# RetNet attention and an MLP mixer on one core: the channel product of batches 1 to 3 by seven quarter products

## The chip, the cores and the metric

The kernel runs on one core of a Trainium2 chip. The metric is the device time of one execution in microseconds, lower is better; the median of three runs of the kernel before is 209.35 us (208.44 to 210.75). The engines are named as the profile names them: PE (matrix products, with PEld for its weight loads), DVE (vector), ACT (scalar), POOL (GpSimd) and SP, which only issues transfers.

## The reference

For 4 batches, 8 heads, 768 positions and a head size of 64, a recurrent attention with decay, then a mixer over tokens and one over channels:

```python
for t in range(S):                                   # S = 768
    state = gamma * state + einsum('bhd,bhe->bhde', k[:, :, t], v[:, :, t])
    y[:, :, t] = scale * einsum('bhd,bhde->bhe', q[:, :, t], state)
x  = y as (4, 768, 512)
h  = relu(x^T @ w_tok1) @ w_tok2                     # 768 -> 256 -> 768
u  = x + h^T
out = u + relu(u @ w_ch1) @ w_ch2                    # 512 -> 1536 -> 512
```

Inputs and output are float32; the products run in float16 with float32 sums.

## The kernel before

The recurrence is done by chunks of 128 positions, six to a batch. Two heads form a pair, and a batch has four pairs. `front(b, p)` is the attention of one pair and its share of the token mixer. It casts k (scaled by the decay, L471 on ACT or L473 on DVE) and q (L480 or L482), turns both so that the head size lies across partitions (for batches 0 and 1 by PE, L506, with copies out of the bank on L515 and L519; for batches 2 and 3 by a transposing transfer on SP, L497), and forms five state products for each of two heads (L542, 64x64 each, in one bank). A scan on DVE (L547) runs the decay over the five chunks, with the factors in the constant `gsc`; its result U has the chunk index innermost. The two heads' diagonal blocks are copied, scaled, into the f16 tile r (L558 on ACT, L560 on POOL). Scores (L579) are masked on DVE (L593), then L607 (state) and L610 (scores) form y. It is scaled into X (L623 on ACT, L627 on DVE), cast (L640), multiplied by w_tok1 (L651) and w_tok2 (L712), added into X (L719 on DVE), cast again (L727) and turned into uT (SP, L736; for batch 1 by PE, L746 and L752). Batch 0 takes a shorter way to uT (L681, L684, L691).

`back(b)` is the channel mixer. `widen(sh)` multiplies half a batch (384 positions) by w_ch1: 12 column tiles of 4 products of 384 columns (L781), each followed by a relu into the f16 tile h2 on ACT (L797). `narrow(sh)` multiplies by w_ch2: for each tile of 128 positions 12 products of 512 columns in one bank (L818; batch 0 adds its token mixer there, L816), then one DVE addition of X and the bank into a tile `o` (L827), which ACT's queue writes out (L833).

Nothing runs in the order in which it is written. Each piece of work is an `Op` with the engines that can do it and a cost for each. `arrange` plays all of them through a plan with these costs, with a model of the transfer rings (`Rings`) and of buffers and PSUM banks, and picks for each engine in turn the ready Op of the highest priority. The plan's order is then recorded, so each engine has a fixed order of instructions; what is waited for at run time follows from the tiles. An Op's `after` holds it back in the plan alone. In gaps of the plan's first 30 us, PE gets filler products of zeros (L881).

Transfers of k and q are issued on SP (L421, L418), those of v (L429) and the weights (L397, in order w_tok1, w_tok2, three thirds of w_ch1, three of w_ch2) on POOL. Eight PSUM banks are shared: 0 to 4 for the fronts of batches 1 to 3, 5 to 7 for their backs; batch 0 has its own ranges.

Of the kernel before, what the change touches and what calls it, by code (L numbers as in the profile page):

```python
# [40 lines left out]
class Rings:  # L41
# [5 lines left out]
    LAND = dict(SP=750, POOL=900, ACT=1500)  # L47
# [37 lines left out]
def arrange(ops, BUFS, BANKS, rank, fixed=None, noise=None):  # L85
# [87 lines left out]
    while left:  # L173
        moved = False
        wake = INF
        for e in ENGINES:
# [5 lines left out]
            for o in w_:  # L182
# [15 lines left out]
                if fixed is not None:  # L198
                    way = way_fix[o.n]
                else:  # L200
                    way = None
                    for w in o.ways:
                        f = max(t, free[w[0]]) + w[2]
                        if way is None or f < way[0] or (f == way[0] and w[0] == e):
                            way = (f, w)
                    if way[1][0] != e:
                        continue
                    way = way[1]
# [49 lines left out]
def kernel(  # L258
# [31 lines left out]
    BUFS = dict(kf=4, qf=3, k16=3, q16=3, v16=6, kT=4, qT=4, U=2, r16=3, am=8, X=3, x16=5, h1=5, u16=3,  # L290
                uT=3, h2=2, o=4)
    BANKS = dict(first=range(0, 7), front=range(0, 5), back=range(5, 8), back0=range(3, 8))
    XB = 2
# [33 lines left out]
    gsc = const_p.tile([P, NP, (NC - 1) * D], FP, name="gsc")  # L327
# [32 lines left out]
    def emit():  # L360
        nc.vector.memset(mask1, 1.0)
        nc.vector.memset(gsc, 0.0)
        for p in range(NP):
            g = gsc[:, p].rearrange("p (e c) -> p e c", c=NC - 1)
            nc.vector.memset(g[:D, :, 1:], g128[2 * p])
            nc.vector.memset(g[D:, :, 1:], g128[2 * p + 1])
    gp_op = prep("DVE", 4200, emit, prio=(0, -1, 1))
# [13 lines left out]
    NW = 3  # L381
    FW = NF // NW
    wc1 = [const_p.tile([P, NP, FW * P], F16, name=f"wc1_{i}") for i in range(NW)]
    wc2 = [const_p.tile([P, FW, C], F16, name=f"wc2_{i}") for i in range(NW)]
# [4 lines left out]
    def request(prio, cost, emit, dma, takes=()):  # L389
        o = Op(ops, prio, [("POOL", cost, cost, emit)], [], takes, dma=dma,  # L390
               after=queue[-6:-5], behind=queue[-1] if queue else None)
# [14 lines left out]
    rows = []  # L406

    def load(b, p):
        got = []
        for tag, src in (("kf", k), ("qf", q)):  # L410
            s = Slot(tag)
            wide = b < XB and tag == "qf"

            def emit(s=s, src=src, tag=tag, wide=wide):
                t = tile_of(s, [P, 2, NC, D], FP)
                r = src[b, 2 * p:2 * p + 2]
# [3 lines left out]
                else:  # L420
                    nc.sync.dma_start(out=t, in_=r.rearrange("h (c p) d -> p (h c) d", p=P))  # L421
            o = Op(ops, (0, b, p), [("SP", 500, 500, emit)], [], [s], dma=(16, 66) if wide else (96, 18),
                   after=rows[-4:-3] if b == 0 else rows[-2:-1], behind=rows[-1] if rows else None)
            rows.append(o)
            got.append((s, o))
        s = Slot("v16")

        def emit(s=s):
            nc.gpsimd.dma_start(out=tile_of(s, [P, 2, NC, D], F16),  # L429
                                in_=v[b, 2 * p:2 * p + 2].rearrange("h (c p) d -> p (h c) d", p=P))  # L430
        got.append((s, request((0, b, p), 1030, emit, (96, 17), [s])))
        loads[b, p] = got

    def front(b, p):
# [24 lines left out]
        (KF, kd), (QF, qd), (V, vl) = loads[b, p]  # L459
# [33 lines left out]
        def turn(src, dst, dep):  # L493
            if b >= XB:
# [40 lines left out]
        ST, US, RS = Slot(FA), Slot("U"), Slot("r16")  # L535
        EC = (NC - 1) * D

        def emit():
            st = tile_of(ST, [P, 512], FP)[:, :EC].rearrange("p (e c) -> p c e", c=NC - 1)
            for c in range(NC - 1):  # L540
                for j in range(2):
                    nc.tensor.matmul(st[j * D:(j + 1) * D, c], K.tile[:, c, j], V.tile[:, j, c],  # L542
                                     start=True, stop=True)
        pp = op(one("PE", (350, 500), emit), kl + [vl, two_before], [ST], [K, V])

        def emit():
            nc.vector.tensor_tensor_scan(out=tile_of(US, [P, EC], FP), data0=gsc[:, p], data1=ST.tile[:, :EC],  # L547
                                         initial=0.0, op0=ALU.mult, op1=ALU.add)
        prev = op(one("DVE", (740, 820), emit), [pp, gp_op], [US], [ST])

        def emit(e, j):
# [4 lines left out]
            u = US.tile[r].rearrange("p (e c) -> p c e", c=NC - 1)  # L556
# [5 lines left out]
        r0 = op(either(lambda e, f=emit: f(e, 0), ACT=(365, 470), POOL=(400, 470)),  # L562
                [prev, r16_op], [RS], [US])
        r1 = op(either(lambda e, f=emit: f(e, 1), ACT=(365, 470), POOL=(400, 470)),
# [16 lines left out]
        if first:  # L581
            a2 = [op(one("PE", (290, 420), lambda f=emit, h=hf: f([h])), [kt[hf], qt[hf], two_before],
                     A4[2 * hf:2 * hf + 2], [KT, QT]) for hf in range(2)]
        else:
            a2 = 2 * [op(one("PE", (460, 590), lambda f=emit: f([0, 1])), kt + qt + [two_before], A4, [KT, QT])]
# [146 lines left out]
        if b >= XB:  # L732
# [27 lines left out]
    def back(b):  # L760
# [10 lines left out]
        def widen(sh):  # L771
            H2 = H2s[sh]
            rel = []
            for ft in range(NF):
# [11 lines left out]
                for part in cuts:  # L786
# [3 lines left out]
                            [uT_done[b, p, sh] for p in ps_] + [wops["c1", ft // FW], c1],  # L790
# [13 lines left out]
        def narrow(sh):  # L804
            H2, rel = H2s[sh], rels[sh]
            for i in range(HC):
                A, O = Slot(BA), Slot("o")
                last = None
                t = slice((sh * HC + i) * P, (sh * HC + i + 1) * P)
                for f0 in range(0, NF, 2):  # L810
                    def emit(f0=f0, i=i, A=A, H2=H2, t=t):
# [5 lines left out]
                        for ft in range(f0, f0 + 2):  # L817
                            nc.tensor.matmul(A.tile, H2.tile[:, ft, i * P:(i + 1) * P],  # L818
                                             wc2[ft // FW][:, ft % FW],
# [5 lines left out]
                def emit(sh=sh, i=i, A=A, O=O):  # L825
                    o = tile_of(O, [P, C], FP)
                    nc.vector.tensor_tensor(o, X.tile[:, sh * HC + i], A.tile, ALU.add)  # L827
                ad = op(one("DVE", (606, 690), emit), [last] + [x_done[b, p, sh] for p in range(NP)],
                        [O], [A, X])

                def emit(sh=sh, i=i, O=O):
                    t0 = (sh * HC + i) * P
                    nc.scalar.dma_start(out=out[b, t0:t0 + P, :], in_=O.tile)  # L833
# [80 lines left out]
```

## Time and profile before

| | |
|---|---|
| median of 3 runs | 209.35 us (208.44 to 210.75) |
| the profiled execution | 210.22 us, of which the profile's span is 208.5 |
| PE, DVE, ACT, POOL busy | 197.6, 104.7, 103.3, 62.9 us |
| narrow product, L818 | 288 products of 128x512 |
| widening, L781 | 384 products of 128x384 |
| states, L542 | 160 products of 128x64 |
| final addition, L827 | 24 of 128x512 on DVE, 683 ns each |
| scan, L547 | 16 of 128x320 on DVE, 814 ns each |
| HBM | 26.74 MB read, 6.29 MB written |

In the profile an engine's busy time is the time in which it had an instruction under way. A product's duration (379 ns for 512 columns) is longer than its distance from the next in an unbroken stream, since products overlap; the chain of work in order of time shows that distance. Times of stages are counted from the span's start.

### The profile page before, as it was taken

How to read it: one execution, taken by the hardware profiler on the slowest of the kernel's cores; microseconds unless marked ns; L12 is line 12 of the kernel's file. 1: busy time of each engine (PE TensorE's matmuls, PEld its weight loads, DVE VectorE, ACT ScalarE, POOL GpSimd, SP SyncE). 2: the span in 40 equal slices, each digit the busy share in tenths (PEclk: the TensorE clock that was granted, in tenths of full speed). 3: DMA queues.
4: the chain of work that ended last, by engine and by line, in shares of the span. 5: the costliest groups of instructions: out<-in, count | busy, mean ns of one | idle time of the engine just before them, and what ended most of it. 6: DMA issues, size and time to landing. Idle time of an engine off the chain costs nothing.

```text
span 208.5 us, 4578 instructions
## 1 busy us (share of the span) xinstructions
PE 197.6 (95%) x1856; PEld 121.9 (58%) x1856; DVE 104.7 (50%) x218; ACT 103.3 (50%) x210; POOL 62.9 (30%) x100
## 2 busy tenths in 40 slices
PE   7987499999999999999999999999999999999992
PEld 3655387666456677575557666666755545545540
DVE  6988642401468997863747658748441021021021
ACT  2676457677415876356306673566304704704600
POOL 8644362705123457253414225133410000000000
PEclk9999969999999999999999999999999999999998
DMA  6999999999999999999999999972053012012012
GB/s 166 202 198 189 213 197 229 197 226 190 195 173 198 170 197 165 179 213 216 145 225 152 205 133 214 247 177 41 0 119 108 3 50 101 3 50 101 0 50 101
DMA packets 91156, 30.96 MB, mean 148 GB/s; under 512 B 81920, under 2 KB 88064, under 8 KB 91136
## 3 DMA queue, kind: packets, MB, share of 16 engines
q1 hardware_dynamic: 58624, 17.31, 52.9%
q0 software_dynamic: 29056, 7.08, 34.5%
q10 hardware_dynamic: 3456, 6.29, 8.4%
q8 instruction: 14, 0.23, 0.5%
q14 instruction: 6, 0.05, 0.1%
HBM read 26.74 MB, written 6.29 MB: 158 GB/s over the span
## 4 chain that ended last, share of the span: by engine, by line
PE 81%; DMA 10%; DVE 3%; ACT 1%; POOL 1%; SPq 1%; issue 1%; DVEq 0%; POOLq 0%; ACTq 0%
PE bank L781 29%; PE bank L818 29%; DMA qf<-in_q_dram 10%; PE bank L651 5%; PE bank L712 3%; PE bank L579 3%; PE bank L542 2%; PE bank L610 2%; PE bank L607 2%; PE bank L506 2%; PE bank L681 1%; PE bank L816 1%; DVE am L593 1%; POOL r L560 1%; DVE U L547 1%; ACT r L558 1%
## 5 line engine op out<-in xcount | busy, mean ns | idle before, releaser
L797 ACT ACTIVATE h<-bank 128x384 f16<-128x384 f32 x96 | 46.5, 490 | 52.7 <-PE bank L781 27.6
L818 PE MATMUL bank<-wc,h 128*128 128x512 f16 x288 | 68.6, 379 | 0.0
L781 PE MATMUL bank<-uT,wc 128*128 128x384 f16 x384 | 67.7, 326 | 0.0
L781 PEld LDWEIGHTS <-wc 128*128 128x128 f16 x384 | 35.9, 98 | 22.9
L818 PEld LDWEIGHTS <-h 128*128 128x128 f16 x288 | 26.4, 98 | 27.8
L827 DVE TENSOR_TENSOR o<-X,bank 128x512 f32<-128x512 f32 x24 | 16.4, 683 | 47.2 <-PE bank L818 46.9
L593 DVE TENSOR_TENSOR am<-bank,mask 128x384 f16<-128x384 f32 x64 | 31.8, 549 | 16.5 <-PE bank L579 16.3
L558 ACT ACTIVATE r<-U 64x320 f16<-64x320 f32 x24 | 18.8, 782 | 10.7 <-DVE U L547 10.3
L640 POOL CAST x<-X 128x384 f16<-128x384 f32 x26 | 13.3, 512 | 32.9 <-DVE X L627 21.9
L719 DVE TENSOR_TENSOR X<-X,bank 128x384 f32<-128x384 f32 x24 | 12.2, 549 | 12.1 <-PE bank L712 12.0
L482 POOL CAST q<-qf 128x768 f16<-128x768 f32 (+1 forms) x13 | 10.6, 812 | 21.8 <-DMA qf<-in_q_dram 21.8
L429 POOL DMA_DIRECT2D v<-in_v_dram x16 | 16.6, 1039 | 1.9 <-PE bank L610 1.5
L727 POOL CAST u<-X 128x384 f16<-128x384 f32 x21 | 10.2, 508 | 22.6 <-DVE X L719 22.6
L623 ACT ACTIVATE X<-bank,gy 128x192 f32<-128x192 f32 x28 | 10.2, 416 | 10.3 <-PE bank L610 10.2
L610 PE MATMUL bank<-v,am 128*128 128x64 f16 x192 | 15.2, 195 | 0.1
L610 PEld LDWEIGHTS <-am 128*128 128x128 f16 x192 | 12.9, 99 | 3.4 <-DVE am L593 0.7
L547 DVE TENSOR_TENSOR_SCAN U<-gsc,bank 128x320 f32<-128x320 f32 x16 | 13.0, 814 | 1.8 <-PE bank L542 1.4
L881 PE MATMUL bank<-zero 128*128 128x384 f16 x52 | 12.6, 390 | 1.2 <-DVE zero L339 1.2
L651 PE MATMUL bank<-x,wt 128*128 128x128 f16 x192 | 13.7, 224 | 0.0
L651 PEld LDWEIGHTS <-wt 128*128 128x128 f16 x192 | 12.2, 101 | 2.2
L627 DVE TENSOR_TENSOR X<-bank,gyw 128x384 f32<-128x384 f32 x18 | 9.9, 552 | 6.5 <-PE bank L610 6.4
L607 PE MATMUL bank<-r,qT 128*128 128x128 f16 x80 | 12.7, 222 | 0.1
(60 smaller groups left out, 161.7 us busy)
## 6 DMA issues: line engine op xcount, KB each, us to landing
kf<-in_k_dram SPq DMA_DIRECT2D x16, 384.0 KB, 9.1
qf<-in_q_dram SPq DMA_DIRECT2D x16, 384.0 KB, 9.6
out_dram<-o ACTq DMA_DIRECT2D x24, 256.0 KB, 3.3
v<-in_v_dram POOLq DMA_DIRECT2D x16, 192.0 KB, 11.9
wc<-in_moe_w_ch_dram POOLq DMA_DIRECT2D x6, 512.0 KB, 19.8
wt<-in_moe_w_tok_dram POOLq DMA_DIRECT2D x2, 384.0 KB, 19.6
kT<-k SPq DMA_TRANSPOSE x8, 5.9
qT<-q SPq DMA_TRANSPOSE x8, 6.2
```

The costliest lines, as they stand in the source:

```text
L429: nc.gpsimd.dma_start(out=tile_of(s, [P, 2, NC, D], F16), in_=v[b, 2 * p:2 * p + 2].rearrange("h (c p) d -> p (h c) d", p=P))
L547: nc.vector.tensor_tensor_scan(out=tile_of(US, [P, EC], FP), data0=gsc[:, p], data1=ST.tile[:, :EC], initial=0.0, op0=ALU.mult, op1=ALU.add)
L558: nc.scalar.mul(RS.tile[r, :, r], u, g128[2 * p + j])
L593: nc.vector.tensor_tensor(am, src, m, ALU.mult)
L607: nc.tensor.matmul(o, QT.tile[:, c * P:(c + 1) * P], R[:, c - 1], start=True, stop=False)
L610: nc.tensor.matmul(o[:, j * D:(j + 1) * D], AM[2 * hf + j].tile[:, i], V.tile[:, j, c], start=(c == 0), stop=(c == 0 or j == 1))
L640: (nc.vector if e == "DVE" else nc.gpsimd).tensor_copy(X16.tile[:, half(hf)], X.tile[:, half(hf), pc])
L651: nc.tensor.matmul(acc[:, jt * P:(jt + 1) * P], wt1[:, i, jt * P:(jt + 1) * P], X16.tile[:, i], start=(i == 0), stop=(i == NC - 1))
L781: nc.tensor.matmul(acc[:, :SH], w[:, ct, (ft % FW) * P:(ft % FW + 1) * P], UT.tile[:, ct, sh * SH:(sh + 1) * SH], start=(ct == 0), stop=(c ...
L797: nc.scalar.activation(H2.tile[:, ft], A.tile[:, :SH], AF.Relu)
L818: nc.tensor.matmul(A.tile, H2.tile[:, ft, i * P:(i + 1) * P], wc2[ft // FW][:, ft % FW], start=(ft == 0 and b > 0), stop=(ft == NF - 1))
L827: nc.vector.tensor_tensor(o, X.tile[:, sh * HC + i], A.tile, ALU.add)
```

## The change

It has six parts.

1. Seven products. For batches 1 to 3, `narrow7(i0, i1)` takes two tiles of 128 positions together. With their h2 tiles cut in two along the 1536 channels and w_ch2 cut in two both ways, the result is a 2x2 by 2x2 product of blocks, done by seven block products with sums of blocks ahead and behind (Winograd's form of Strassen's method). A block product is 6 products of 256 columns (new L873). Ahead stand four sums of h2 blocks (f16, 128x768, DVE or POOL, new L858), and once in the kernel four sums of w_ch2 blocks (`wsum`, 128x1536, new L979). Behind stand eleven additions of 128x256 (new L889) and one copy on ACT (new L907) for a pair of tiles. Two block products share a bank, and the second is issued after the first has been read.
2. States. The five chunks' products are of the whole array, both heads' k by both heads' v (128x128, new L540); the blocks off the diagonal are formed and not used. They take two banks. The scan is replaced by a copy and four dependent multiply-adds of 128x128 (new L546, L548), U has the chunk index outermost, and `gsc` (3.3 us of memsets) gives way to one column a pair.
3. Outputs are summed in place in X, and written from there; the tiles `o` are gone.
4. w_ch1 comes in pieces of 2, 2, 4 and 4 column tiles instead of 4, 4 and 4. In the plan alone, the first k of batch 1 is held back until the third piece has landed.
5. Buffers: v16 4 (was 6), x16 4 (5), uT 2 (3). Banks of the fronts 0 to 5, of the backs 4 to 7, so that two are shared.
6. The plan's costs: later landings, 400 ns added on DVE after 30 us where it chooses between engines, and a few costs of products.

By the order of the recorded instructions this moves, beside what the parts name: k casts from DVE to ACT (DVE 14 to 8), copies kT likewise (8 to 1), the scaling of y into X (DVE 18 to 7), and each uT transposition on SP one or two places back. PE's 92 widening products of batch 0 stand in one stretch, with batch 1's first turns behind them instead of between them.

The core of the difference, cut:

```diff
-    LAND = dict(SP=750, POOL=900, ACT=1500)
+    LAND = dict(SP=900, POOL=1300, ACT=1500)
...
-                        f = max(t, free[w[0]]) + w[2]
+                        f = max(t, free[w[0]]) + w[2] + (400 if w[0] == "DVE" and t > 30000 else 0)
...
-    BANKS = dict(first=range(0, 7), front=range(0, 5), back=range(5, 8), back0=range(3, 8))
+    BANKS = dict(first=range(0, 7), front=range(0, 6), back=range(4, 8), back0=range(3, 8))
+    SEVEN = (1, 2, 3)
...
+    CW = [2, 2, 4, 4]
+    wsum = const_p.tile([P, 4, K2, N2], F16, name="wsum")
...
             for c in range(NC - 1):
-                for j in range(2):
-                    nc.tensor.matmul(st[j * D:(j + 1) * D, c], K.tile[:, c, j], V.tile[:, j, c],
-                                     start=True, stop=True)
+                nc.tensor.matmul(st[c // 4][:, c % 4 * P:(c % 4 + 1) * P],
+                                 K.tile[:, c].rearrange("p h d -> p (h d)"), V.tile[:, :, c], start=True, stop=True)
...
-            nc.vector.tensor_tensor_scan(out=tile_of(US, [P, EC], FP), data0=gsc[:, p], data1=ST.tile[:, :EC],
-                                         initial=0.0, op0=ALU.mult, op1=ALU.add)
+            nc.vector.tensor_copy(u[:, 0], ST[0].tile[:, :P])
+            for c in range(1, NC - 1):
+                nc.vector.scalar_tensor_tensor(out=u[:, c], in0=u[:, c - 1], scalar=gp[:, p:p + 1],
+                                               in1=ST[c // 4].tile[:, c % 4 * P:(c % 4 + 1) * P],
+                                               op0=ALU.mult, op1=ALU.add)
...
+            sums = [(lambda: h(hb, tb, 0), lambda: h(hb, tb, 1), ALU.add, rb, None),
+                    (lambda: HS.tile[:, 0], lambda: h(ha, ta, 0), ALU.subtract, ra[:K2], 0),
+                    (lambda: h(ha, ta, 0), lambda: h(hb, tb, 0), ALU.subtract, ra[:K2] + rb[:K2], None),
+                    (lambda: h(ha, ta, 1), lambda: HS.tile[:, 1], ALU.subtract, ra[K2:], 1)]
...
+                    for j in range(K2):
+                        nc.tensor.matmul(acc[:, half], l[:, j], r[:, j], start=(j == 0), stop=(j == K2 - 1))
...
+            p1 = product(0, lo, lambda: h(ha, ta, 0), w(0, lo), ra[:K2] + cw)
+            u0 = op(either(emit, ACT=act(N2), DVE=dve(N2)), [p1], [US], [banks[0]])
+            p2 = product(2, lo, lambda: h(ha, ta, 1), w(1, lo), ra[K2:] + cw)
+            y1 = add(part(x0, lo), part(x0, lo), u(0), [u0] + xd, [US, X])
+            o11 = add(part(x0, lo), part(x0, lo), acc(2, lo), [p2, y1], [X, banks[2]])
+            p6 = product(0, hi, lambda: HS.tile[:, 1], t(1), [sm[1], u0] + wsums)
+            u2 = add(u(1), u(0), acc(0, hi), [u0, p6], [US, banks[0]])
+            p5 = product(1, lo, lambda: HS.tile[:, 0], t(0), [sm[0]] + wsums)
+            y3 = add(part(x1, lo), part(x1, lo), u(1), [u2] + xd, [US, X])
+            p4 = product(2, hi, lambda: h(hb, tb, 1), t(3), rb[K2:] + wsums + [o11])
+            u4 = add(u(2), u(1), acc(1, lo), [u2, p5], [US, banks[1]])
+            z3 = add(part(x1, lo), part(x1, lo), acc(2, hi), [p4, y3], [X, banks[2]])
+            p7 = product(1, hi, lambda: HS.tile[:, 2], t(2), [sm[2], u4] + wsums)
+            y2 = add(part(x0, hi), part(x0, hi), u(2), [u4] + xd, [US, X])
+            y4 = add(part(x1, hi), part(x1, hi), u(2), [u4] + xd, [US, X])
+            o21 = add(part(x1, lo), part(x1, lo), acc(1, hi), [z3, p7], [X, banks[1]])
+            o22 = add(part(x1, hi), part(x1, hi), acc(1, hi), [y4, p7], [X, banks[1]])
+            p3 = product(0, lo, lambda: HS.tile[:, 3], w(1, hi), [sm[3], u2] + cw)
+            o12 = add(part(x0, hi), part(x0, hi), acc(0, lo), [y2, p3], [X, banks[0]])
...
+        if b in SEVEN:
+            widen(0)
+            narrow7(0, 1)
+            widen(1)
+            narrow7(2, 3)
+            narrow7(4, 5)
```

## Prediction

> **What bounds the kernel now.** I read the busy shares first, then the chain that ended last, then the busy time stage by stage, then the groups for durations. From the page's first two parts:
>
> ```profile
> PE 197.6 (95%) x1856; PEld 121.9 (58%) x1856; DVE 104.7 (50%) x218; ACT 103.3 (50%) x210; POOL 62.9 (30%) x100
> ...
> DVE  6988642401468997863747658748441021021021
> ...
> PEclk9999969999999999999999999999999999999998
> ```
>
> PE is busy 95% of the span at full clock but for one slice and the last; DVE is near full in slices 12 to 18 only. The chain of work in order of time (start, length, what):
>
> ```profile
> 2.58 21.59 DMA qf<-in_q_dram x2
> ...
> 89.77 0.40 PE bank L542 x10
> 90.17 0.76 PE bank L781 x4
> 90.93 0.67 PE bank L651 x12
> ...
> 158.08 7.80 PE bank L781 x48
> 165.88 7.77 PE bank L818 x36
> ...
> 204.81 0.02 issue
> 204.83 0.69 DVE o L827
> ```
>
> It gives the start (transfers of k and q until 24.2) and PE's rates in an unbroken stream: 7.77/36 = 0.216 us for 512 columns, 7.80/48 = 0.1625 for 384, 0.67/12 = 0.056 for 128, and 0.040 for a 64x64 state product. Count times rate for every line of PE's order gives 173.45 us of work from the last score product of batch 0 (26.05) to PE's end (204.64), which took 178.59. So PE lost only 5.14 us after the start. I cut that at the points where PE's order changes character; the stages' busy times are:
>
> ```profile
> 36.16:53.86 17.70, 17.70 (x141) 10.91 (x139) 4.21 (x9) 12.71 (x28) 7.18 (x8) 1.00 1.35 203
> 53.86:87.95 34.09, 34.02 (x402) 21.70 (x400) 27.72 (x53) 17.92 (x35) 13.69 (x21) 1.00 1.59 180
> 87.95:151.87 63.92, 63.35 (x689) 41.26 (x688) 39.61 (x77) 33.76 (x69) 21.94 (x37) 1.00 1.04 165
> 151.87:208.50 56.63, 52.92 (x283) 27.28 (x280) 9.21 (x14) 17.66 (x36) 0.97 (x2) 0.99 0.18 62
> ```
>
> The columns are length, then PE, weight load, DVE, ACT, POOL. Work against elapsed: 26.05 to 36.16, 8.55 of 10.11 (lost 1.56); widening of batch 0, 17.50 of 17.70 (0.20); batch 0's narrow product over batch 1's attention, 32.84 of 34.09 (1.25); batches 2 and 3's attention over the products of 1 and 2, 61.78 of 63.92 (2.14); pure products, 52.78 of 52.77 (0). What PE has to do sets the time, if the others keep up. DVE is 81% full in the third stage and 62% in the fourth.
>
> ```profile
> L827 DVE TENSOR_TENSOR o<-X,bank 128x512 f32<-128x512 f32 x24 | 16.4, 683 | 47.2 <-PE bank L818 46.9
> L593 DVE TENSOR_TENSOR am<-bank,mask 128x384 f16<-128x384 f32 x64 | 31.8, 549 | 16.5 <-PE bank L579 16.3
> L558 ACT ACTIVATE r<-U 64x320 f16<-64x320 f32 x24 | 18.8, 782 | 10.7 <-DVE U L547 10.3
> L482 POOL CAST q<-qf 128x768 f16<-128x768 f32 (+1 forms) x13 | 10.6, 812 | 21.8 <-DMA qf<-in_q_dram 21.8
> L547 DVE TENSOR_TENSOR_SCAN U<-gsc,bank 128x320 f32<-128x320 f32 x16 | 13.0, 814 | 1.8 <-PE bank L542 1.4
> ```
>
> **PE's work after.** Batches 1 to 3 issued 216 products of 512 columns: 216 x 0.216 = 46.66. They become 9 pairs of tiles x 7 products x 6 = 378 of 256 columns. No row has 256; it lies between 0.056 (128) and 0.1625 (384). The stream is linear in the columns (0.216, 0.1625 and 0.056 fit 0.0024 + 0.000417 per column), so 0.109: 41.20, saving 5.46. The 128-column row changes its weights at every product and still streams at 0.056, so the 162 extra weight loads hide; at 0.13 the saving would be gone. States: 10 x 0.040 becomes 5 x 0.056 in 16 places, 1.92, of which 1.44 lies after 26.05. Three filler products fewer there: 0.49. Sum 7.39: the work after 26.05 falls to 166.06, by stage 7.72, 15.94, 33.28, 63.16 and 45.96.
>
> **DVE's work after.** From the instruction order, with these prices. A 256-column add of a bank: 683 and 549 ns for 512 and 384 columns give 147 + 1.047 per column, so 0.415, and 0.39 in sequence (64 masks of 549 ns took 31.8 us, so neighbours overlap by 0.05). 80 of them, 31.2; 18 adds of 512 go (12.3). The scan (814) becomes a copy and four dependent steps of 128 columns, 0.281 each plus a semaphore row of 0.02: 1.5, so +0.69 in 16 places. An f16 sum of 768: between 0.555 (the copy kT of 128x768 f16, L519) and 0.95 (the line above, one element at a time); I take the copy, the nearest in type. 20 on DVE, 11.1, and three weight sums of 1536 at 0.96. To ACT and POOL move six k casts, seven kT, two qT and eleven X evictions (13 us). In all 104.7 becomes about 127. By stage: the third 28.1 of 33.3 (84%, was 81%), the fourth 56.9 of 63.2 (90%, was 62%), the last two pairs 9.6 of 9.2 us of products.
>
> [...]
>
> **POOL and ACT.** POOL takes 16 sums of 768 from two f16 tiles. The cast of 768 f32 elements reads the same bytes in 0.83 (the half-size one left out), and two such passes are 1.65; I take 1.0, near the row with equal bytes. With nineteen 256-column adds (0.36 to 0.72), POOL rises from 63 to about 91. ACT gains casts, copies and X, and loses on r if the now contiguous read is cheaper (782 down to 0.57, the k cast of 128x384 at 609 scaled to 320; at worst 782): 103 to about 125, 26.5 of 33.3 in the third stage.
>
> [...] No row of before has a two-input operation on POOL.
>
> **New waits.** Each pair uses three banks twice, so p6 waits for ACT's copy of p1's half, p4 for DVE's o11, p3 for u2, p7 for u4; behind the waiting product stands all of PE. In the last two pairs, followed step by step with these prices, the products stall 0.2 to 0.4, and DVE ends 0.4 to 0.5 later behind PE than its one add of 0.69 now: 0.9 lost (0.3 to 3). In the fourth stage I scale the third stage's loss, 1.25 in 34.09 with 19% of DVE idle, to 10% idle: 1.25/34.09 x 1.9 x 63.2 = 4.4, say 4.3 (2 to 11). Third stage: 1.5 (1 to 4). Start: 1.6 (0.6 to 3), since the last pair's state steps (1.5) stand ahead of its masks on DVE while the last q is cast and turned. Widening: 0.2 (0 to 2).
>
> **Costed at nothing.** Dropping the gsc memsets (3.3 us of DVE) frees time before the first state at 10.2, under the loads. Smaller c1 pieces: POOL's queue is backlogged (pieces issued at 7.5, 12.3, 17.5 landed at 30.5, 34.6, 38.0), so splitting them, or issuing them behind r and q, leaves the landing alone; c2's last third landed at 48.8 and is wanted at about 51, 2.5 us of cover, and if POOL's three r steps push it past that, up to 2 us. On SP each uT transpose stands one or two places later. The scores of batches 2 and 3 would start at about 87 to 144, and their turned q landed, before, 1.8 us (batch 2's last pair) to 5 us ahead of these times; if landings slip by more, PE waits. v with four buffers: v issues wait for PE on POOL, some 8 us ahead of need. Fewer uT and output sums in place: their slots were free 8 us or more before.
>
> **Sum.** 26.05 + 166.06 + 8.5 lost (1.6+0.2+1.5+4.3+0.9) + 3.86 (PE's end to the span's, before) = 204.5, against 208.5. The profiled run took 210.22, 1.72 beyond its span: 206.2, a gain of 4.0. The median of the runs shown is 209.35, so I forecast 205.3.
>
> **Rivals.** (1) PE's saving arrives whole: losses stay at 5.1. For: the third stage lost 1.25 with DVE at 81%. Against: every product of a pair waits on DVE or ACT. Span 201.1, time 202.0. (2) DVE becomes the bound in the fourth stage: f16 sums at 0.95, no overlap (0.44 an add, 0.55 a mask), state steps 1.8. Then DVE's list there is 9 x 0.95 + 34 x 0.44 + 32 x 0.55 + 7 x 1.8 + 24 others x 0.56 = 67 us, and POOL's 1.65 us sums hold it up for 5 more: 72 for 63.2 of products, 9 lost, and 3 each in the third stage, the start and the end: 18 lost, 215.7, less 0.87: 214.8. It decides from 12.5 us lost in all (5.14 + 7.39). For: 90% is the fullest stage that this kernel would have. Against: the third stage. (3) Transfers and transposes of batches 2 and 3 land 4 us later than before, since SP's waits hang on casts of fuller engines: 4 us more lost, 209.3.
>
> **How the numbers follow.** Forecast 0.46, rival 1 0.24, rival 2 0.15, rival 3 0.15. About 1% (2.1 us) is what a measurement of this kernel can tell from no change. The forecast and rival 1 give faster by over 1% (below 207.3): 0.70; rival 3 the same, 0.15; rival 2 slower, 0.15. The range runs from 201.0, 1 us less lost than in rival 1, to 211.5, short of rival 2: 10% beyond it above and 8% below. The forecast alone: 203 to 207.
>
> **What would show it.** Right: 378 products 0.109 apart when unbroken, PE's work 166 after the start, DVE 85% to 92% full from batch 1's widening to the end of attention, PE waits named after DVE. Wrong: products of 256 columns further apart than 0.12; f16 sums near 0.95; POOL sums above 1.3; PE waiting for transposed q.

## The result, and the profile after

The changed kernel takes 228.41 us (median of four runs, 227.78 to 229.62) against 209.12 us for the kernel before beside it (208.44 to 210.75): a ratio of 1.092, with a 95% interval of 1.084 to 1.100. It is slower by 9%, where 205.3 us was forecast. Some executions run 1 to 2% longer at a lower granted clock (beside the first experiment the kernel before took 207.87 to 210.41 us at 0.992 to 1.000 in eight executions, 211.71 to 212.75 at 0.980 to 0.984 in five); every ratio here leaves them out, while the times in us beside the ratios are medians of all executions.

The first lines of the page of the changed kernel: busy time, then DVE and PE's granted clock in forty slices, then the chain that ended last by engine.

```profile
PE 198.3 (87%) x1941; PEld 138.9 (61%) x1941; DVE 148.3 (65%) x331; ACT 118.8 (52%) x261; POOL 110.2 (49%) x141
...
DVE  7499920013989984468967999577916972441993
...
PEclk9999999999999999799999999999999969999799
...
PE 50%; DMA 17%; DVE 16%; POOL 7%; issue 5%; ACT 3%; POOLq 1%; DVEq 0%; ACTq 0%
```

DVE was busy 148 us where 127 had been forecast, POOL 110 where 91 had, and the chain is PE's for only half of its length. The busy times of the last four stages (length, then PE, weight load, DVE, ACT, POOL, then the clock) put the loss at the end:

```profile
33.61:51.74 18.13, 16.28 (x106) 9.56 (x103) 1.11 (x2) 12.62 (x27) 2.87 (x4) 1.00 1.25 209
51.74:88.49 36.75, 34.33 (x393) 22.59 (x392) 29.78 (x68) 22.81 (x50) 19.17 (x27) 1.00 1.25 172
88.49:164.03 75.54, 68.54 (x771) 51.52 (x769) 57.92 (x124) 42.37 (x99) 42.28 (x57) 0.98 0.88 141
164.03:226.90 62.87, 50.99 (x356) 35.62 (x352) 35.35 (x60) 19.45 (x41) 25.23 (x20) 0.94 0.17 57
```

Elapsed time less the forecast's own PE work gives what each stage lost (the last one up to PE's end at 222.74):

| stage | work | lost, forecast | lost, measured |
|---|---|---|---|
| start, from the last scores at 24.84 | 7.72 | 1.6 | 1.05 |
| widening of batch 0 | 15.94 | 0.2 | 2.19 |
| narrow product of 0 over attention of 1 | 33.28 | 1.5 | 3.47 |
| attention of 2 and 3 over products | 63.16 | 4.3 | 12.38 |
| pure products | 45.96 | 0.9 | 12.75 |
| sum | 166.06 | 8.5 | 31.84 |

24.84 + 166.06 + 31.84 + 4.16 (PE's end to the span's) is the span of 226.9. The start came 1.2 us earlier than forecast, but that is chance: with PE's order the same up to there, these score products stand anywhere from 24.59 to 26.86 in the profiles of the experiments. The work was taken as counted, and the loss is 23 us larger.

What PE's block products (L873) waited for, by the last releaser (us in total, times, longest):

```profile
PE bank L873 <- DVE hs L858: 4.5, 2, 2.2
PE bank L873 <- DVE X L889: 3.3, 4, 1.6
PE bank L873 <- DVE us L889: 3.0, 2, 2.2
...
PE bank L873 <- POOL hs L858: 0.9, 1, 0.9
```

PE stood still for DVE's sums and additions, 10.8 us, and hardly for POOL's sums themselves, 0.9.

The timeline of DVE and of POOL in the last stage (start, length, engine, line, tiles) shows what DVE did in the first of these long waits:

```profile
172.23 0.56 DVE L858 TENSOR_TENSOR hs<-h 128x768 f16<-128x768 f16 x1 [6.95 <-ACT h L799]
172.85 1.72 DVE L889 TENSOR_TENSOR X<-X,us 128x256 f32<-128x256 f32 x1
174.49 1.98 DVE L858 TENSOR_TENSOR hs<-hs,h 128x768 f16<-128x768 f16 x1
176.40 0.41 DVE L889 TENSOR_TENSOR X<-X,bank 128x256 f32<-128x256 f32 x1
176.73 1.66 DVE L858 TENSOR_TENSOR hs<-h,hs 128x768 f16<-128x768 f16 x1
178.31 1.98 DVE L858 TENSOR_TENSOR hs<-h 128x768 f16<-128x768 f16 x1
...
172.34 1.94 POOL L858 TENSOR_TENSOR hs<-h 128x768 f16<-128x768 f16 x1 [6.45 <-ACT h L799]
174.25 1.81 POOL L858 TENSOR_TENSOR hs<-h,h 128x768 f16<-128x768 f16 x1
176.02 1.95 POOL L858 TENSOR_TENSOR hs<-hs,h 128x768 f16<-128x768 f16 x1
178.05 1.83 POOL L858 TENSOR_TENSOR hs<-h,hs 128x768 f16<-128x768 f16 x1
```

The sum at 172.23, before POOL begins, takes 0.56. An addition of 256 columns that takes 0.41 at 176.40, where one operand is a bank, takes 1.72 at 172.85, where both are SBUF tiles and POOL is in a sum. Each long DVE operation ends 0.3 to 0.5 us after one of POOL's sums: 174.57 after 174.28, 176.47 after 176.06, 178.39 after 177.97, 180.29 after 179.88. PE stood idle for 2.24 us ahead of 176.53 for a sum and 2.15 us ahead of 181.01 for a running sum. Behind two of its three gaps of over 2 us the granted clock was lower, 0.69 from 181 to 184 us and 0.67 from 213 to 218 (0.94 over the stage); blocks of six products that follow each other every 0.65 us elsewhere did so there at up to 1.28. By these starts an estimated 3 of the 12.75 us lost went that way. That the gaps cause it is not shown by a run.

### The profile page after: what moved, and what is told of

It is laid out like the page before. It is cut to its first block, busy times and chain, and to the rows that moved or that the text cites. A ratio compares the mean times of both kernels' runs of the same rounds, so it can differ in the third digit from the quotient of the medians.

```text
span 226.9 us, 4970 instructions
## 1 busy us (share of the span) xinstructions
PE 198.3 (87%) x1941; PEld 138.9 (61%) x1941; DVE 148.3 (65%) x331; ACT 118.8 (52%) x261; POOL 110.2 (49%) x141
## 4 chain that ended last, share of the span: by engine, by line
PE 50%; DMA 17%; DVE 16%; POOL 7%; issue 5%; ACT 3%; POOLq 1%; DVEq 0%; ACTq 0%
PE bank L783 24%; DMA wc<-in_moe_w_ch_dram 8%; PE bank L873 6%; PE bank L820 6%; DVE hs L858 6%; DMA qf<-in_q_dram 5%; DVE X L889 5%; POOL hs L858 4%; DMA v<-in_v_dram 4%; PE bank L714 2%; PE bank L653 2%; DVE U L548 2%; PE bank L581 2%; PE bank L612 1%; ACT h L799 1%
## 5 line engine op out<-in xcount | busy, mean ns | idle before, releaser
L873 PEld LDWEIGHTS <-hs 128*128 128x128 f16 x216 | 21.3, 102 | 15.8 <-DVE hs L858 5.0
L873 PE MATMUL bank<-wsum,hs 128*128 128x256 f16 x162 | 23.7, 288 | 6.5 <-DVE hs L858 4.5
L858 DVE TENSOR_TENSOR hs<-h 128x768 f16<-128x768 f16 x11 | 12.1, 1096 | 24.0 <-ACT h L799 24.0
L889 POOL TENSOR_TENSOR X<-X,us 128x256 f32<-128x256 f32 x19 | 15.3, 815 | 20.2 <-DVE us L889 10.6
L548 DVE SCALAR_TENSOR_TENSOR U<-U,gp,bank 128x128 f32<-128x128 f32 x64 | 22.3, 348 | 3.4
L873 PEld LDWEIGHTS <-h 128*128 128x128 f16 x162 | 16.3, 102 | 6.7 <-issue 3.7
L820 PE MATMUL bank<-wc,h 128*128 128x512 f16 x72 | 19.0, 379 | 0.0
L889 DVE TENSOR_TENSOR X<-X,bank 128x256 f32<-128x256 f32 x45 | 16.9, 413 | 2.5 <-POOL X L889 1.6
L470 ACT ACTIVATE k<-kf,gk 128x384 f16<-128x384 f32 x24 | 14.0, 613 | 3.2 <-DMA kf<-in_k_dram 2.5
L979 DVE TENSOR_TENSOR wsum<-wc 128x1536 f16<-128x1536 f16 x2 | 1.9, 959 | 19.5 <-DMA wc<-in_moe_w_ch_dram 19.5
L873 PE MATMUL bank<-wc,h 128*128 128x256 f16 x108 | 14.3, 281 | 0.0
```

Of the source, the lines that this page charges most:

```text
L548: nc.vector.scalar_tensor_tensor(out=u[:, c], in0=u[:, c - 1], scalar=gp[:, p:p + 1], in1=ST[c // 4].tile[:, c % 4 * P:(c % 4 + 1) * P], o ...
L858: (nc.vector if e == "DVE" else nc.gpsimd).tensor_tensor(HS.tile[:, j], x(), y(), f)
L873: nc.tensor.matmul(acc[:, half], l[:, j], r[:, j], start=(j == 0), stop=(j == K2 - 1))
L889: (nc.vector if e == "DVE" else nc.gpsimd).tensor_tensor(dst(), a_(), b_(), ALU.add)
```

## The experiments

The kernel before was run beside every group; ratios are to it. "PE's stall" is the time from 26 us to PE's last product less the count of products times their distances in an unbroken stream, fillers counted as stall: 5.3 us before, 31.3 after.

**The same order, POOL's two-input work made on DVE.** The plan is untouched, so each engine's place in the order stays; only the 36 instructions with two SBUF tiles that the plan gave to POOL are issued on DVE.

```diff
-                    (nc.vector if e == "DVE" else nc.gpsimd).tensor_tensor(HS.tile[:, j], x(), y(), f)
+                    nc.vector.tensor_tensor(HS.tile[:, j], x(), y(), f)
...
-                    (nc.vector if e == "DVE" else nc.gpsimd).tensor_tensor(dst(), a_(), b_(), ALU.add)
+                    nc.vector.tensor_tensor(dst(), a_(), b_(), ALU.add)
...
-                (nc.vector if e == "DVE" else nc.gpsimd).tensor_tensor(wsum[:, j], x, y, ALU.subtract)
+                nc.vector.tensor_tensor(wsum[:, j], x, y, ALU.subtract)
```

> The plan and its order are kept; the 36 instructions of two SBUF tiles that it gave to POOL (16 f16 sums, 19 additions into X, one weight sum) are issued on DVE at the same places. Theory 1 (shared access: while POOL adds two SBUF tiles, an addition of two SBUF tiles on DVE does not go on and ends only after POOL's): every f16 sum on DVE takes 0.55 to 0.58 us (1.1 to 2.0 for most in the changed kernel) and every X plus us 0.41; PE loses 4 to 8 us between batch 1's widening and the end of attention instead of 12.4, and 3 to 8 after it instead of 12.8; time 213 to 219. Theory 2 (hand-over: PE waits for DVE at the second use of each bank, because DVE is full of short steps): DVE gets 17.7 us more (16 x 0.56, 19 x 0.41, 0.96), so the losses stay or grow; time 226 to 234. Theory 3 (the loss comes from the other parts): 225 to 230.

Measured: 215.3 us, ratio 1.027 (1.017 to 1.036), PE's stall 17.4 us. DVE was given 36 instructions more, and the kernel became 13 us faster, within theory 1's range. PE's order is the same, so the stages can be set side by side: the last three lose 2.0, 9.0 and 4.1 us here instead of 3.5, 12.4 and 12.8; the 9.0 is above the 4 to 8 that theory 1 gave. The groups of DVE (line, form, count, busy, mean ns), first after, then here:

```profile
L889 DVE TENSOR_TENSOR X<-X,us 128x256 f32<-128x256 f32 x17 | 12.8, 755 | 0.4
L858 DVE TENSOR_TENSOR hs<-h 128x768 f16<-128x768 f16 x11 | 12.1, 1096 | 24.0 <-ACT h L799 24.0
L858 DVE TENSOR_TENSOR hs<-h,hs 128x768 f16<-128x768 f16 x4 | 6.4, 1592 | 0.4 <-POOL hs L858 0.4
```

```profile
L889 DVE TENSOR_TENSOR X<-X,us 128x256 f32<-128x256 f32 x36 | 14.3, 424 | 0.1
L858 DVE TENSOR_TENSOR hs<-h 128x768 f16<-128x768 f16 x15 | 8.1, 554 | 23.8 <-ACT h L799 23.8
L858 DVE TENSOR_TENSOR hs<-h,hs 128x768 f16<-128x768 f16 x9 | 5.0, 552 | 0.0
```

With POOL's two-input work gone, DVE's sums take 0.55 us on average and the 36 additions 0.42; after, 20 sums took 25.5 us and 17 additions 12.8, some 20 us more than at those prices. DVE's 148.3 us without these 20 are 128, near the 127 forecast.

**The operations alone and in pairs.** A kernel without the computation; it writes zeros.

```diff
+    for fv, nv, fp, np_ in ((v_sum, 6, None, 0), ..., (v_sum, 8, p_sum, 8), (v_bank, 24, p_sum, 6), (v_copy, 8, p_sum, 8), ...):
+        for i in range(max(nv, np_)):
+            if i < np_: fp(i)
+            if i < nv: fv(i)
+        sync()
```

> A kernel of its own that leaves the whole computation out and writes zeros: rows of DVE and POOL instructions on tiles of zeros, first each alone, then both engines side by side. f16 sum of two SBUF tiles 128x768, float32 addition of two SBUF tiles 128x256, float32 addition of an SBUF tile and a bank 128x256, float32 copy 128x768 within SBUF on DVE; f16 sum 128x768, float32 addition 128x256 and a cast of one tile 128x768 on POOL. Theory 1: alone 0.56, 0.41, 0.41 on DVE and 1.65, 0.72, 0.82 on POOL; beside POOL's sums, DVE's sums and its additions of two SBUF tiles last 1.5 to 2.0 each, the addition with a bank stays at 0.41; beside POOL's casts of one tile nothing changes by more than 10%. The copy within SBUF is open: 0.55 if only two inputs count, up to 2 if it also uses what POOL uses. Theory 2: no duration beside the other engine is over 10% longer than alone.

The timeline of DVE and POOL; L297 is the f16 sum of 128x768 on DVE, L300 the addition of two SBUF tiles, L303 that of a tile and a bank, L306 a one-input copy, L309 the f16 sum on POOL, L312 POOL's addition, L315 POOL's cast of one tile:

```profile
8.09 2.90 DVE L297 TENSOR_TENSOR vd<-a,b 128x768 f16<-128x768 f16 x6
16.65 2.91 DVE L306 COPY vf<-x 128x768 f32<-128x768 f32 x6
20.45 9.61 POOL L309 TENSOR_TENSOR pd<-c,d 128x768 f16<-128x768 f16 x6
...
35.37 4.68 POOL L315 CAST pd<-z 128x768 f16<-128x768 f32 x6
...
40.33 12.47 DVE L297 TENSOR_TENSOR vd<-a,b 128x768 f16<-128x768 f16 x8
40.92 14.96 POOL L309 TENSOR_TENSOR pd<-c,d 128x768 f16<-128x768 f16 x8
...
72.27 8.03 DVE L303 TENSOR_TENSOR vf<-x,bank 128x256 f32<-128x256 f32 x24
72.59 9.61 POOL L309 TENSOR_TENSOR pd<-c,d 128x768 f16<-128x768 f16 x6
...
82.48 12.47 DVE L306 COPY vf<-x 128x768 f32<-128x768 f32 x8
...
98.31 8.99 DVE L297 TENSOR_TENSOR vd<-a,b 128x768 f16<-128x768 f16 x10
98.89 9.67 POOL L312 TENSOR_TENSOR pf<-z,w 128x256 f32<-128x256 f32 x10
...
118.73 10.72 DVE L297 TENSOR_TENSOR vd<-a,b 128x768 f16<-128x768 f16 x12
119.30 8.81 POOL L315 CAST pd<-z 128x768 f16<-128x768 f32 x8
```

Alone a sum takes 0.48 us on DVE (2.90/6) and 1.60 on POOL. Side by side they go in step: DVE's eight sums take 1.56 each (12.47/8), the first of them begun before POOL's, and POOL's sum 1.87 instead of 1.60 (14.96/8). In the changed kernel's timeline above, the four sums on POOL have beside them four operations of DVE with two SBUF tiles, of 1.66 to 1.98. A one-input copy between SBUF tiles is held in the same way (12.47/8). The addition with a bank is not held (24 in 8.03 us, 0.335 each), and POOL's sums beside it stay at 1.60. POOL's additions of 256 columns hold DVE for less: 0.97 us a pair (9.67/10). Theory 1 holds but for one part: beside POOL's casts, which read a single tile, it expected no change. A cast takes 1.10 us there instead of 0.78 (8.81/8 and 4.68/6), and by the starts and ends, with 0.48 a sum before and after the casts, an estimated eight of DVE's twelve sums fall into the eight casts, one for one.

So the sums and the copy wait for POOL, and the addition with a bank does not. A pair of sums takes 1.87 us, somewhat less than one after the other (1.60 + 0.48). What in the hardware makes them wait is not shown.

**Only the sums off POOL.** As the first experiment, but the 19 additions X+us stay on POOL.

```diff
-                    (nc.vector if e == "DVE" else nc.gpsimd).tensor_tensor(HS.tile[:, j], x(), y(), f)
+                    nc.vector.tensor_tensor(HS.tile[:, j], x(), y(), f)
...
-                (nc.vector if e == "DVE" else nc.gpsimd).tensor_tensor(wsum[:, j], x, y, ALU.subtract)
+                nc.vector.tensor_tensor(wsum[:, j], x, y, ALU.subtract)
```

> The changed kernel with the 16 sums hs and the one sum wsum that its plan gave to POOL made on DVE, and only the 19 additions X+us left on POOL. Theory 1 (DVE is held whenever POOL runs a two-input operation, so the loss goes with the time that POOL runs them): POOL ran sums for some 33 us and additions for 15 us, and the whole of it cost 228.4 - 215.3 = 13.1 us, so the additions alone leave 15/48 of that, 4 us: 218 to 221 us. Theory 1b (only the long sums hurt, since an addition of 0.7 us holds DVE no longer than DVE's own work takes): 214.5 to 217 us. Theory 1c (the additions, which stand between two products of one bank, hurt as much as the sums): 222 to 226 us.

Measured: 212.9 us, 1.021 (1.015 to 1.027), stall 15.5 us, below each of the three ranges, nearest to 1b. The whole gain comes from the 16 sums and the one wsum; the additions on POOL cost nothing that can be measured, and moving them to DVE too was no better (215.3). Theories 1 and 1c fall: the loss does not go with POOL's time but with its long operations (1.64 to 1.95 us a sum in the changed kernel, 0.82 an addition). PE's order is again the same, and the last three stages lose 2.0, 6.4 and 4.4 us instead of 3.5, 12.4 and 12.8.

**The plan without POOL.** The plan itself is not offered POOL for this work.

```diff
-                sm.append(op(either(emit, DVE=(470, 550), POOL=(1000, 1060)),
+                sm.append(op(either(emit, DVE=(470, 550)),
...
-                    ways["POOL"] = (600, 660)
+                    pass
```

> As the run before, but the plan itself no longer has POOL as a choice for the sums and additions of two SBUF tiles, so DVE's and PE's orders are made for it. Theory 1: 211 to 218, f16 sums on DVE at 0.55 to 0.58. Theory 2: 224 or more. Theory 3: 225 to 230.

Measured: 212.7 us, 1.016 (1.008 to 1.024), stall 14.4 us, within theory 1's range. With POOL's two-input work gone the kernel is still slower than before, though TensorE has 7.4 us less to do.

**What is left: the sums, or DVE's load?** In this last version, in the same order on every engine, first the 36 sums are left out, then the 54 additions to and of the running sums; the output is another one in both.

```diff
-                    nc.vector.tensor_tensor(HS.tile[:, j], x(), y(), f)
+                    pass
...
-            p5 = product(1, lo, lambda: HS.tile[:, 0], t(0), [sm[0]] + wsums)
+            p5 = product(1, lo, lambda: h(hb, tb, 0), t(0), [sm[0]] + wsums)
...
```

```diff
                 def emit(e):
+                    if US in uses:
+                        return
```

> The version with all sums planned on DVE (212.7 us; PE 14.4 us without useful work after the first 26 us, against 6.3 us without seven products), in the same order on every engine, but with the 36 sums hs left out: the four products that read a sum read a quarter of h in its place, so the output is another one. TensorE runs the same 1941 matmuls. Theory S (PE waits for the sums, as in the two gaps of 0.74 us of the last stage, and DVE is too full in batches 1 and 2): the stalls fall to some 6 to 8 us: 203.5 to 206 us. Theory D (only DVE's load counts; the sums are 20 us of it, the additions into and onto the running sums 22 us, and taking away either does the same): 204 to 208 us here and the same within 1.5 us where those additions are left out. Theory R (PE waits for the running sums, which stand between two products of a bank): 210.5 to 213 us.

> The same version and order, but with the 54 additions to and of the running sums (us+bank and X+us; 22 us of DVE) left out, while the sums hs and the 45 additions X+bank stay; the output is another one. Theory S: DVE has time but each pair still waits for its first sum: 208.5 to 211 us. Theory D: as without the sums, 204 to 208 us. Theory R: 203.5 to 206 us.

Measured: 206.6 us, 0.985 (0.978 to 0.991), without the sums; 206.9 us, 0.985 (0.978 to 0.992), without the additions; stalls of 8.7 and 9.0 us. The sums are 20 us of DVE by their groups and the additions 22; DVE's busy time falls from 142.4 by 16.6 and 17.3 us, and the kernel gains 6 us either way, as theory D said. R falls, and S in that the sums are no dearer than the additions. Each run also takes links out of the chains in which PE waits, so that the load alone makes the 6 us is argued, not shown. The stage from batch 1's widening to 157, of the version with everything on DVE and of the two:

```profile
86.96:156.94 69.98, 66.04 (x771) 50.73 (x769) 57.70 (x140) 40.51 (x97) 26.23 (x44) 1.00 1.03 157
```

```profile
87.00:157.00 70.00, 67.93 (x789) 52.43 (x790) 50.47 (x126) 41.90 (x100) 26.76 (x48) 1.00 1.09 169
```

```profile
87.00:157.00 70.00, 67.99 (x791) 52.62 (x790) 50.78 (x118) 42.52 (x102) 26.03 (x45) 1.00 1.02 163
```

DVE falls from 82% to 72% and 73% busy (57.70, 50.47 and 50.78 of 70), and PE does 18 to 20 products more in the same 70 us.

**No seven products.**

```diff
-    SEVEN = (1, 2, 3)
+    SEVEN = ()
```

> The changed kernel with batches 1 to 3 narrowed by 12 products of 512 columns as before; states, sums in place, c1 pieces, buffers and plan costs as changed. Theories 1 and 2: PE's work after the start is 166.1 + 5.5 = 171.5, losses about 1.1, 2.2, 3.5 and 3 by stage and none after attention, start 24.8 and tail 3.9: span 210, time 209 to 213. Theory 3: 220 or more.

Measured: 209.1 us, 1.000 (0.995 to 1.005), stall 6.3 us. The seven products carry the whole loss of 9%; the other five parts together are worth nothing that can be measured.

**c1 in three pieces again,** in the version without seven products.

```diff
-    CW = [2, 2, 4, 4]
-    CF = [0, 2, 4, 8]
+    CW = [4, 4, 4]
+    CF = [0, 4, 8]
```

> The changed kernel without seven products (SEVEN = (), 209.1 us) and with c1 in three pieces of four again. Theory P (the four pieces cost the wait of 1.44 us for the third piece at 39.9 us, which the three pieces do not have): 207.3 to 208.3 us, ratio to before 0.990 to 0.996. Theory Q (the weights land no sooner in three pieces, since the queue ahead of them is the same; the wait only moves to the first or the second piece): 208.6 to 209.8 us, ratio 0.997 to 1.003.

Measured: 208.2 us, 0.997 (0.994 to 1.000), stall 5.6 us. The gap of 1.44 us in the widening of batch 0, which stood before the last piece (landed at 41.5 us), is gone. But the interval reaches into both theories, and 0.9 us of the lead is lost again behind 80 us, half of it by 88. A small gain at best.

**Seven products for batch 3 alone,** all on DVE, with four pieces of c1 and then with three.

```diff
-    SEVEN = (1, 2, 3)
+    SEVEN = (3,)
```

> Seven products only for batch 3 (SEVEN = (3,)), every sum and addition of them planned and made on DVE. Theory A: a pair of row blocks gains 0.61 us of PE (24 x 0.216 against 42 x 0.109) wherever DVE has time, and the loss of the version with all sums on DVE (212.7 us) comes from batches 1 and 2, where DVE has none. Three pairs gain 1.8 us against the version without seven products (209.1 us), less some 0.5 to 1 us of waits for the first sum: 207.5 to 208.7 us, ratio to before 0.992 to 0.998. Theory B: the product of sums never pays, since PE waits for the first sum in each pair (0.74 and 0.74 us were such gaps in the last stage) and for an addition (0.98 us): 209 to 211 us, ratio 1.000 to 1.008.

> Both edits together: seven products for batch 3 alone on DVE, and c1 in three pieces. If theories A and P hold, the gains add: 206 to 207.5 us, ratio 0.985 to 0.992. If only one of them holds: 207.3 to 208.7 us. If neither: 209 to 211 us.

Measured: 209.5 us, 1.003 (1.000 to 1.006), and 208.5 us, 0.999 (0.996 to 1.003). The first falls into theory B's range; neither shows a gain clear of noise, though DVE has time in the last stage. PE's timeline at the end of the second shows where the 1.8 us went:

```profile
195.49 0.83 PE L873 MATMUL bank<-wsum,hs 128*128 128x256 f16 x6 [0.58 <-DVE hs L858]
...
200.41 0.82 PE L873 MATMUL bank<-wc,hs 128*128 128x256 f16 x6 [0.82 <-DVE us L889]
```

Counted from one stream to the next, these two waits are 0.74 and 0.98 us, together 1.7. They are the only two in the batch, and they stand where two pairs of seven products end the kernel, with no other products to put between.

**The last pair by plain products,** with three pieces of c1.

```diff
             widen(1)
             narrow7(2, 3)
-            narrow7(4, 5)
+            narrow(1, (1, 2))
```

> Seven products for the first two of batch 3's three pairs of row blocks alone, on DVE; the last pair by the twelve products of before, and c1 in three pieces. Theory A (what took the gain in the last stage are the two waits at its end, 0.74 us for a sum and 0.98 us for a running sum; with a plain pair at the end they go, and 2 x 0.61 us stays of the gain against 208.2 us): 206.7 to 207.4 us, ratio to before 0.989 to 0.994. Theory B (a pair by seven products waits for its sum wherever it stands): 207.9 to 209 us, ratio 0.996 to 1.002.

Measured: 207.2 us, 0.990 (0.983 to 0.996). The time is in theory A's range, and the timeline agrees with it: over the same end PE has plain products (L820) between the blocks, and none waits. The gain over the version without any seven products (0.997, 0.994 to 1.000) is not clear of noise, since the two intervals overlap.

```profile
193.75 1.47 PE L873 MATMUL bank<-wc,h 128*128 128x256 f16 x12
195.06 0.59 PE L820 MATMUL bank<-wc,h 128*128 128x512 f16 x2
195.49 1.47 PE L873 MATMUL bank<-wsum,hs 128*128 128x256 f16 x12
196.80 1.03 PE L820 MATMUL bank<-wc,h 128*128 128x512 f16 x4
197.66 0.82 PE L873 MATMUL bank<-wsum,h 128*128 128x256 f16 x6
```

**The old states, and the new states alone.** First the scan and the 64x64 products in the version without seven products; then only the new states in the kernel before.

```diff
-        pp = op(one("PE", (285, 440), emit), kl + [vl, two_before], ST, [K, V])
+        pp = op(one("PE", (350, 500), emit), kl + [vl, two_before], [ST], [K, V])
...
-        prev = op(one("DVE", (1480, 1560), emit), [pp, gp_op], [US], ST)
+        prev = op(one("DVE", (740, 820), emit), [pp, gp_op], [US], [ST])
```

> The changed kernel without seven products (209.1 us, ratio to before 1.000), with the states of the kernel before: ten products of 64x64 per pair of heads in one bank and one scan on DVE. Theory 1 (the states by whole-array products save PE 16 x (0.400 - 0.280) = 1.9 us, 1.4 us of it after the first 26 us, and PE is the bound): 210 to 211.3 us, ratio 1.004 to 1.011. Theory 2 (what PE saves is lost again, since the five steps on DVE take 1.6 us where the scan takes less, and PE waits for r): 208.5 to 209.5 us, ratio 0.997 to 1.002. Theory 3 (the five steps cost more than PE saves): 207 to 208.3 us, ratio 0.990 to 0.996.

> The kernel of before with the new states alone (five whole-array products into two banks, a copy and four steps on DVE, r from the diagonal blocks); its planner, buffers, c1 in three pieces and direct products stay. Theory 1 (the states save 3 us by themselves: 1.9 us of PE and a cheaper r, 0.46 us on ACT or POOL against 0.78): ratio 0.981 to 0.989. Theory 2 (PE's time alone, 1.4 us as forecast): 0.990 to 0.996. Theory 3 (in this order the steps on DVE are late and nothing is left; the 1.6% is owed to the changed order, in which the old states would stand badly): 0.998 to 1.006.

Measured: 212.8 us, 1.016 (1.008 to 1.024), with the old states in the changed kernel; 212.9 us, 1.012 (1.007 to 1.016), with the new states in the old kernel. Both lie above every range that was expected. The states are worth 1.6% to the one and cost 1.2% in the other. So what they are worth belongs to the order around them: the changed loads, banks and buffers without the new states lose about what the states bring. Which of these it is stays open; the kernel before with the new states and the new banks has no result.

**Buffers and constants of before.** Buffers in the version without seven products; the plan's constants in the version with two pairs.

```diff
-    ... v16=4 ... x16=4 ... uT=2
+    ... v16=6 ... x16=5 ... uT=3
```

```diff
-    LAND = dict(SP=900, POOL=1300, ACT=1500)
+    LAND = dict(SP=750, POOL=900, ACT=1500)
-                        f = max(t, free[w[0]]) + w[2] + (400 if w[0] == "DVE" and t > 30000 else 0)
+                        f = max(t, free[w[0]]) + w[2]
```

> The version without seven products and with c1 in three pieces (ratio to before 0.997), with the buffers of before restored, for which the missing products leave room (v16 6, x16 5, uT 3). Theory 1 (fewer buffers hold up loads and casts, and cost most of the 3 us that the states save): ratio 0.983 to 0.990, 205 to 207 us. Theory 2 (the buffers cost nothing; the loss sits elsewhere): ratio 0.994 to 1.000, 207.5 to 209 us.

> The version with seven products for two pairs of batch 3 (ratio to before 0.990), with the planner's constants of before (landing times 750 and 900 ns, nothing added to DVE's finish). Theory 1 (the changed constants send casts to POOL that DVE would have had sooner, as at the end of the third stage, where PE stands still for 1.3 us before the transposes of u): ratio 0.980 to 0.986. Theory 2 (no difference): 0.987 to 0.993. Theory 3 (the changed constants are the better ones for this order): 0.995 to 1.005.

Measured: 209.0 us, 0.993 (0.988 to 0.998), with the buffers, between the theories and not to be told from 0.997; 206.2 us, 0.982 (0.977 to 0.987), with the constants. This is the fastest version: it beats the kernel before by 1.8% and the changed one by 10% (0.982/1.092 is 0.90). Its stall is 4.5 us against 6.9 with the changed constants, but the intervals of the two ratios overlap, and the profile with the changed constants is of that version's slowest execution (209.06 us), which was some 3 us behind already at batch 0's last scores (27.42 against 24.28).

```profile
PE 193.3 (95%) x1814; PEld 124.5 (61%) x1814; DVE 123.8 (61%) x302; ACT 101.9 (50%) x215; POOL 62.5 (31%) x104
```

PE is at 95% again, and ACT has lost 13 us (115.1 us with the changed constants) to DVE. The time is in theory 1's range, but the wait that theory 1 named, PE's for the cast of u on POOL, is still there (1.5 us, 1.2 with the changed constants). How much of the 1.8% the two pairs give, and how much the constants, stays open: this version without any seven products has no result.

## Why the prediction was wrong

**What held.** PE's prices: unbroken products of 256 columns follow each other at 0.109 (the last three blocks of six start at 220.78, 221.43 and 222.09) with a weight load for every product (1941 of each in the kernel), so the extra loads hide, and the work from the last scores on is 166.0 by the run's own count (165.6 after 26 us and 0.44 of score products before) against 166.06. DVE's prices alone: 0.413 for an addition with a bank (0.415 forecast), 0.554 for an f16 sum (0.555). r became cheaper, 0.46 against the 0.57 taken. Rival 3 did not come: no wait of PE of 0.3 us or more is put down to a transposed q.

**The step that failed: DVE's prices were taken as its own.** The forecast's sum has no term for what DVE and POOL cost each other side by side. The forecast of 127 us of DVE and 4.3 and 0.9 us lost in the last two stages rests on DVE operations that run at 0.41 and 0.555 whatever POOL does. In the runs they take up to 1.99 beside a sum on POOL, some 20 us more in all. Taking the sums off POOL gives 228.4 - 212.9, 15.5 us: two thirds of the miss of 23.1.

**POOL's sum, "I take 1.0, near the row with equal bytes".** It measured 1.60 in an unbroken stream and 1.64 to 1.95 in the changed kernel, at and above the upper bound of 1.65. POOL's additions took 0.82 on average, above the text's estimate of 0.36 to 0.72. The two mistakes are one in effect, since DVE is held for about the length of POOL's sum (1.98 us at 174.49, beside a sum of 1.81 and the start of the next). The sign that the text set for being wrong, POOL sums above 1.3, is what the profile shows. Its other sign, f16 sums near 0.95, shows too (1.10 to 1.59 on average), but from another cause than the one meant there, DVE's own rate. The sign set for being right, DVE 85% to 92% full up to the end of attention, did not show: it was 77% (57.92 of 75.54), held operations included.

**The fourth stage's loss, 4.3 "scaled to 10% idle".** With the same order and the sums off POOL that stage loses 6.4, above 4.3 but inside the bounds of 2 to 11, and the last stage 4.4, above its bound of 3. With all of it on DVE the kernel still takes 212.7 us. Leaving either the sums or the running sums' additions out gives 6 us and some 206.7, near the forecast of 205.3. So a DVE at 82% in that stage, with PE waiting for it in chains of sums, costs by these two runs an estimated 6 us in the whole kernel, and the linear scaling from the third stage was too kind. The rival "DVE becomes the bound", at 214.8, came nearest in its mechanism, in that DVE is late. But it made DVE late through slower rates of its own and through waits for POOL's sums, not through operations that POOL holds up, and that its time is near that of the version with all of it on DVE is chance.

**Sums and readings of the text.** Its own terms for DVE add up to 132, not to 127 (104.7 + 31.2 - 12.3 + 11.0 + 11.1 + 2.9 - 13 - 3.3). So that 127 is near the 128 that is left without the held time is in part luck. And the row of DVE before is as full in slices 2 to 4 (988) as in 12 to 18, not in these only.

**Costed at nothing.** The pieces of c1: the last landed at 41.0 where the last third had landed at 38.0, and PE, early by the chance of its start, waited twice for them; 2.19 us were lost in that stage instead of 0.2, of which three pieces give back 0.6 us in the time at best. **The states:** a step takes 0.348, not 0.281, and yet the changed order is faster with them by 1.6% and not by the 1.44 us of PE's time (0.7%), while alone they make the kernel before slower. So their worth was not PE's time, and what it hangs on stays open.

## What to carry to other kernels

Before work with two SBUF inputs is split between DVE and POOL, price it in pairs: here, while POOL was in such an operation, DVE got one done for each of POOL's (an f16 sum of 128x768 took DVE 0.48 us alone and up to 1.99 beside POOL's, which took 1.60 alone), so the slow helper made the fast engine as slow as itself. A cast on POOL did it too, for its shorter time (1.10 us a pair). Before TensorE products are traded for sums, see whether the sums' engine has time and other products stand between a sum and the product that waits for it; here two of nine pairs stood so, without waits, and even their gain is not clear of noise (0.990 against 0.997). DVE at 82% in a chain of short dependent steps was not a spare engine here: the kernel gained 6 us when 20 us of its sums or 22 us of its additions went.

## What was not expected of the hardware

POOL loses too when the two meet: its sum goes from 1.60 to 1.87 us, so that eight sums on each engine took 15.5 us, while sixteen on DVE alone would take 7.7 (16 x 0.48). A one-input copy of 128x768 f32 on DVE between SBUF tiles, 0.485 us alone, is held like a two-input sum (1.56 us on average), though it reads only one tile; an addition of 256 columns that reads a bank is not held at all (0.335 us each in a row of 24 beside POOL's sums). A cast on POOL and a sum on DVE delay each other as well (1.10 us a pair), though the cast reads only one tile. And PE's clock was 0.94 over the last stage of the changed kernel, where it stood idle for 2 us at a time; in the version whose plan has no sums on POOL, with gaps of at most 0.8 us there, it was 0.99; that the gaps lower it is not shown.
